# Second channel layer by seven block products also beside attention, with its sums in the mixing's two rooms

## The chip, the cores and the metric

The kernel runs on one core of one Trainium2 chip. The metric is the device time of one execution in microseconds, and the median of three runs stands for the kernel. One more execution was taken by the hardware profiler; all views and durations come from that one. Engines are PE (TensorE, matmuls), DVE (VectorE), ACT (ScalarE), POOL (GpSimd) and SP (the queue that issues DMAs). All data is fp32.

## What is computed

A masked attention over 4 batches, 8 heads, 768 positions and 64 features per head, then per batch a Fourier mixing and a two-layer network on the 768 x 512 result:

```python
scores = scale * np.matmul(q, k.transpose(0, 1, 3, 2))
scores = np.where(mask, scores, -1000000000.0)      # near blocks, edge blocks, sampled blocks
attn = np.exp(scores - np.max(scores, axis=-1, keepdims=True))
attn = attn / (np.sum(attn, axis=-1, keepdims=True) + 1e-09)
x = np.matmul(attn, v)                               # heads side by side: (4, 768, 512)

X = np.fft.fft(np.fft.fft(x, axis=1), axis=2)
u = x + np.real(X)
un = (u - mu) / np.sqrt(var + 1e-06)
out = u + np.maximum(un @ w_ch1, 0.0) @ w_ch2        # 512 -> 2048 -> 512
```

## The kernel before

**Attention** runs in 96 slots (`slot`), 24 for each batch: 4 pairs of heads, two halves of the 768 queries (384 each), and 6 key blocks of 128 in three slots of two units. For a unit PE makes scores (L578), ACT takes the exponential (L606), DVE multiplies by the mask into a tile `e` (L608), POOL adds `e` into `acc` for the row sums (L638), and PE multiplies `e` by the values two slots later (L652, `sum_up`). There are four `e` tiles and two PSUM banks for scores (pool `ps_s`). In the first batches' slots the mask is added on PE and there is no L608.

**The network of a batch runs while the next batch's attention does.** `begin(b)` makes the steps of batch b by `mixer`: a queue `apart` with the normalization (L761), the folds of the Fourier mixing, its products on PE (`zp`, `pq`), the arrivals in x (L926), the whitening `un` (L951), the transposes `utp` (L992) and the subtractions `right` (L1029); then a queue `late` with the two layers. The layers come in four rounds r. Each is two `quad`s (first layer: 512 of 2048 channels for all 768 tokens, by seven block products, L1075) and six `channels` steps (second layer: one of six blocks of 128 tokens, 4 matmuls of 128x512 at L1240, then one DVE add into x at L1243). For the last batch the second layer has a form of its own (`outputs`).

**A round of seven** replaces the six `channels` steps of a round. Its three token rounds (`round_of`, one for 128 tokens of both halves) each make seven products of 128x256 (L1183) in place of eight such blocks. Before these, `sums_room` takes its tiles and `round_right` makes four differences of weight blocks (128x512, POOL, L1152); for each token round `round_left` makes four sums of hidden blocks (two on DVE at L1168, two on POOL at L1165), ACT copies three partial products out of PSUM (`keep`, L1188), and three of the adds into x run on POOL (`later`, L1196), the rest on DVE (`plus` L1192, the double add L1222). The two open products of a token round, `yz` and `yw`, lie in the banks of the scores (`ps_s`). The sums and differences lie in the four `e` tiles, which attention must have left: `sums_room` calls `drain()`, which does the outstanding value products first.

So a round of seven is chosen only with `state["alone"]`. That is set by `until`, which runs all of `late` to its end when a place needs a batch's x finished (in the slots that follow the first ones of batches 2 and 3, and after the last slot): attention stands still there, and the mixing of the next batch runs in the gaps. Round 3 of a batch is always plain. Of the nine rounds 0 to 2 of batches 0 to 2, five go by seven: all three of batch 0, the third of batch 1, the third of batch 2.

**The order of the work** is made while the program is written out, by a model of each engine's time (`when`, `busy`): a wrong estimate moves an instruction in the order, and nothing at run time. After each step of `late`, `gap` takes steps of `apart` that fit by the model; for a DVE step that is `AHEAD` or `start` (from `state["soon"]`) of lead over PE. Beside attention `slot` takes steps of `late` at a pace `(us - COVER) / left`: `us` is the PE time of what lies in `late`, `left` the slots until attention must stand still, and `COVER` = 100 us is what is kept for that stretch. The mixing's rooms `big0` and `big1` (128 x 1536 fp32 each) hold its folds and, later, parts of its products; they lie unused while a batch's layers run and the next mixing has not begun.

Of the kernel before, what the change touches and what calls it, by code (L numbers as in the profile page):

```python
# [11 lines left out]
FP32 = mybir.dt.float32  # L12
# [5 lines left out]
ALU = mybir.AluOpType  # L18
# [81 lines left out]
def kernel(  # L100
# [14 lines left out]
    nc = tc.nc  # L115
# [862 lines left out]
    def mixer(b, xA, xB):  # L978
# [75 lines left out]
        def quad(p):  # L1054
# [5 lines left out]
            if not last:  # L1060
                if p % 2 == 0:
                    seven[p // 2] = state["alone"] and p // 2 < NF // 4 - 1
                elif seven[p // 2]:
                    state["drain"]()
                    sums_room()
                    for j in (1, 2, 4, 3):
                        round_right(p // 2, j)
# [55 lines left out]
            if last:  # L1123
                for j in ((1, 2), (3, 4))[p % 2]:
                    output_right(p // 4, j, p // 2 % 2)
            elif p % 2 == 1 and seven[p // 2]:
                state["soon"] = 0.4

        seven = {}
        w_t, h_s, kept = {}, {}, {}  # L1130

        def sums_room():

            def cut(t, at, k):
                return t[:, at:at + 2 * HS // 3 * k].rearrange("p (k n) -> p k n", k=k)

            rooms = [ep.tile([P, 2 * HS], FP32, tag="e", name="of") for _ in range(4)]
            w_t[1] = wt_p.tile([P, 2, DH], FP32, tag="wt", name="wt")
            for t, j in zip(rooms, (2, 3, 4)):
                w_t[j] = t[:, 0:2 * DH].rearrange("p (k n) -> p k n", n=DH)  # L1140
            for t, j in zip(rooms, (1, 3, 4)):
                h_s[j] = t[:, 2 * DH:2 * HS].rearrange("p (k n) -> p k n", n=P)
            for i in range(3):
                kept[i] = rooms[3][:, i * DH:(i + 1) * DH]

        def part(r, k, n):
            return w2_sb[:, 4 * r + 2 * k:4 * r + 2 * k + 2, n * DH:n * DH + DH]

        def round_right(r, j):
            a, c = {1: (part(r, 0, 1), part(r, 0, 0)), 2: (part(r, 1, 1), w_t[1]),  # L1150
                    3: (part(r, 1, 1), part(r, 0, 1)), 4: (part(r, 1, 0), w_t[2])}[j]
            nc.gpsimd.tensor_tensor(out=w_t[j], in0=a, in1=c, op=ALU.subtract)  # L1152
            busy("POOL", 1.35)

# [3 lines left out]

        def round_left(m, j):
            a11, a12, a21, a22 = tokens(m)  # L1160
            to, a, c, op = {1: (h_s[1], a21, a22, ALU.add), 2: (a21, h_s[1], a11, ALU.subtract),
                            3: (h_s[3], a22, a21, ALU.subtract),
                            4: (h_s[4], a12, a21, ALU.subtract)}[j]
            if j > 2:
                nc.gpsimd.tensor_tensor(out=to, in0=a, in1=c, op=op)  # L1165
                busy("POOL", 0.75, when["DVE"])
            else:
                tt(out=to, in0=a, in1=c, op=op)  # L1168
                busy("DVE", 0.43)

        def round_of(r, m):

            after = dict(zip(OUT, OUT[1:])).get(m)
            a11, a12, a21, a22 = tokens(m)
# [20 lines left out]
            def later(to, i, at):  # L1195
                nc.gpsimd.tensor_add(out=to, in0=kept[i], in1=to)  # L1196
                busy("POOL", 0.75, at)

            def ahead(*js):
                if after is not None:  # L1200
                    for j in js:
                        round_left(after, j)

            if m == OUT[0]:
                round_left(m, 1)
                round_left(m, 2)
            c_at, at = ps_m.tile([P, 512], FP32, tag="m", name="yc")[:, 0:DH], bank("m")
# [6 lines left out]
            if m == OUT[0]:  # L1214
                round_left(m, 3)
                round_left(m, 4)
            gap(start=0.9)
            k1 = keep(1, u_at, product(u_at, a21, w_t[2], False, k0))
            later(a1, 1, k1)
# [7 lines left out]
            ahead(1, 2, 3, 4)  # L1227
            state["soon"] = 1.6

        def channels(r, half, m):  # L1230

            if seven.get(r):
                round_of(r, m)
                if m == OUT[-1]:
                    for _ in range(T):
                        late.popleft()
                return
            y, at = ps_m.tile([P, DM], FP32, tag="m", name="y"), bank("m")
# [138 lines left out]
        for r in range(0 if last else NF // 4):  # L1377
# [9 lines left out]
    MOST, LEAST = 9.6, 2.5  # L1387
    COVER = 100.0
    AHEAD = 2.2
# [8 lines left out]
    state = {"paired": False, "total": None, "w": 0, "got": 0, "owed": 0.0, "ready": 0.0,  # L1398
             "alone": False, "drain": lambda: None}

    def channel_step():
        late.popleft()[0]()

# [58 lines left out]
    def until(met, alone=False):  # L1462

        state["alone"] = alone
        while not met():
            if late:
                channel_step()
                soon = state.pop("soon", None)
                gap(2.0, start=soon)
            else:  # L1470
                do_apart()
        state["alone"] = False

    def begin(b):


        before, after, rest = mixer(b, x_of[b, 0], x_of[b, 1])
# [303 lines left out]
```

## Time and profile before

| | |
|---|---|
| median of three runs | 1064.9 us (1064.24 to 1064.95) |
| profiled execution: its time, its span | 1066.03 us, 1064.3 us |
| mean granted PE clock | 0.987 |
| scores, L578 and values, L652, PE busy | 155.3 and 146.1 us |
| plain channel steps, L1240, matmuls x336, PE busy | 74.8 + 74.5 us |
| token rounds, L1183, matmuls x420 (15 token rounds) | 15.4 to 15.7 us for each of seven products |
| POOL adds of the row sums, L638, x204 | 211.6 us, some 1.06 us each |
| DVE mask multiply, L608, x88 | 79.9 us, 0.948 us each |

A matmul of the program is two instructions on PE in the trace. The span is from the first to the last instruction; the time of an execution also holds what lies around it. Busy times of matmuls overlap by a few tenths at their ends, so the price of a step is taken from one start to the next. The granted clock says which share of the full rate PE was given; it is 1.00 nearly throughout, and half of that in a few stretches of 3.4 or 6.8 us.

The stretches of the run, from the PE timeline: attention of batches 0 and 1 to some 246 us, the first standstill with all of batch 0's layers to 398, attention beside batch 1's layers to 554, the second standstill to 652, attention beside batch 2's layers to some 800, the third standstill with the last mixing to 908, then the last batch's layers alone.

### The profile page before, as it was taken

How to read it: one execution, taken by the hardware profiler on the slowest of the kernel's cores; microseconds unless marked ns; L12 is line 12 of the kernel's file. 1: busy time of each engine (PE TensorE's matmuls, PEld its weight loads, DVE VectorE, ACT ScalarE, POOL GpSimd, SP SyncE). 2: the span in 40 equal slices, each digit the busy share in tenths (PEclk: the TensorE clock that was granted, in tenths of full speed). 3: DMA queues.
4: the chain of work that ended last, by engine and by line, in shares of the span. 5: the costliest groups of instructions: out<-in, count | busy, mean ns of one | idle time of the engine just before them, and what ended most of it. 6: DMA issues, size and time to landing. Idle time of an engine off the chain costs nothing.

```text
span 1064.3 us, 13217 instructions
## 1 busy us (share of the span) xinstructions
PE 1026.7 (96%) x4594; PEld 572.3 (54%) x4594; DVE 708.7 (67%) x1287; ACT 382.5 (36%) x781; POOL 328.3 (31%) x365
## 2 busy tenths in 40 slices
PE   8999999999999998899999999799999999999996
PEld 4333345445766853444444764353445764578575
DVE  6898795877776566754668476765447736675663
ACT  6978765563222214342430223333221221210210
POOL 1000183556733404545561222645440401000000
PEclk9999999999999999999999999999999999899998
DMA  7857422220000002212120001311000002000001
GB/s 211 229 170 225 107 46 45 45 46 15 1 1 1 1 20 69 38 38 32 35 54 0 1 1 39 67 28 24 8 15 1 1 1 57 3 1 1 1 17 47
DMA packets 120549, 46.32 MB, mean 44 GB/s; under 512 B 108172, under 2 KB 113562, under 8 KB 120474
## 3 DMA queue, kind: packets, MB, share of 16 engines
q1 hardware_dynamic: 119222, 44.66, 17.6%
q10 hardware_dynamic: 1220, 0.72, 0.3%
q8 instruction: 38, 0.62, 0.2%
q14 instruction: 37, 0.30, 0.1%
q0 software_dynamic: 32, 0.01, 0.0%
HBM read 36.72 MB, written 6.29 MB: 40 GB/s over the span
## 4 chain that ended last, share of the span: by engine, by line
PE 84%; DVE 5%; ACT 4%; POOL 2%; issue 2%; DMA 1%; SPq 1%; ACTq 0%; DVEq 0%; POOLq 0%
PE z L1075 15%; PE y L1240 13%; PE s L578 12%; PE o L652 10%; PE yp L1075 7%; PE yy L1308 7%; PE xp L1075 4%; PE yz L1183 3%; PE yw L1183 2%; PE yc L1183 2%; PE zp L856 2%; PE s L588 1%; POOL acc L638 1%; ACT e L598 1%; PE sp L719 1%
## 5 line engine op out<-in xcount | busy, mean ns | idle before, releaser
L638 POOL TENSOR_TENSOR acc<-acc,e 128x384 f32<-128x384 f32 x158 | 162.6, 1062 | 97.0 <-DVE e L608 77.9
L578 PE MATMUL s<-qT,kT 64*128 64x384 f32 x768 | 155.3, 519 | 7.6 <-ACT e L598 5.2
L652 PE MATMUL o<-e,vr 128*64 128x384 f32 x768 | 146.1, 508 | 5.0 <-DVE oT L660 5.0
L638 POOL TENSOR_TENSOR acc<-e 128x384 f32<-128x384 f32 x46 | 49.0, 1084 | 202.4 <-ACT e L598 126.0
L578 PEld LDWEIGHTS s<-qT,kT 64*128 64x128 f32 x768 | 64.7, 188 | 86.5 <-ACT e L598 23.1
L608 DVE TENSOR_TENSOR e<-s,mask 128x768 f32<-128x768 f32 x88 | 79.9, 948 | 46.2 <-ACT s L606 35.6
L606 ACT ACTIVATE s<-s 128x768 f32<-128x768 f32 x88 | 66.8, 791 | 106.1 <-PE s L578 105.7
L598 ACT ACTIVATE e<-s 128x768 f32<-128x768 f32 x104 | 79.0, 809 | 49.0 <-PE s L588 36.5
L1075 PE MATMUL z<-unT,t 128*128 128x384 f32 x256 | 93.4, 488 | 1.6 <-DVE hA L1080 1.6
L652 PEld LDWEIGHTS o<-e,vr 128*64 128x64 f32 x768 | 48.5, 139 | 77.0 <-issue 67.5
L1080 DVE TENSOR_TENSOR hA<-z,hA 128x384 f32<-128x384 f32 x64 | 35.6, 557 | 70.0 <-PE z L1075 70.0
L1084 ACT ACTIVATE hA<-hA 128x384 f32<-128x384 f32 x64 | 33.5, 523 | 123.7 <-DVE hA L1080 123.7
L1240 PE MATMUL y<-w_sb,hA 128*128 128x512 f32 x168 | 74.8, 595 | 0.0
L1240 PE MATMUL y<-w_sb,hB 128*128 128x512 f32 x168 | 74.5, 595 | 0.0
L1196 POOL TENSOR_TENSOR x<-of,x 128x256 f32<-128x256 f32 x45 | 34.9, 783 | 123.2 <-ACT of L1188 83.4
L1075 PEld LDWEIGHTS z<-unT,t 128*128 128x128 f32 x256 | 48.3, 190 | 36.9 <-DVE hA L1080 4.0
L1243 DVE TENSOR_TENSOR x<-y,x 128x512 f32<-128x512 f32 x42 | 29.0, 691 | 57.3 <-PE y L1240 57.3
L1084 ACT ACTIVATE hB<-hB 128x384 f32<-128x384 f32 x64 | 33.5, 523 | 87.2 <-DVE hB L1080 87.2
L1240 PEld LDWEIGHTS y<-w_sb,hB 128*128 128x128 f32 x168 | 31.2, 190 | 38.2 <-issue 38.2
L1240 PEld LDWEIGHTS y<-w_sb,hA 128*128 128x128 f32 x168 | 31.1, 190 | 37.5 <-issue 36.7
L1075 PE MATMUL xp<-unT,w_sb 128*128 128x384 f32 x128 | 49.0, 506 | 0.0
L1075 PE MATMUL z<-t,w_sb 128*128 128x384 f32 x128 | 46.6, 487 | 0.2 <-DVE e L608 0.2
(235 smaller groups left out, 1728.5 us busy)
## 6 DMA issues: line engine op xcount, KB each, us to landing
wraw<-in_moe_w_ch_dram SPq DMA_DIRECT2D x32, 512.0 KB
vr<-in_v_dram SPq DMA_DIRECT2D x30, 192.0 KB
qb<-in_q_dram SPq DMA_DIRECT2D x44, 96.0 KB
kb<-in_k_dram SPq DMA_DIRECT2D x44, 96.0 KB
x<-oT SPq DMA_DIRECT2D x192, 12.0 KB
out_dram<-x SPq DMA_DIRECT2D x11, 252.0 KB
out_dram<-x SPq DMA_DIRECT2D x18, 128.0 KB
qr<-in_q_dram SPq DMA_DIRECT2D x24, 64.0 KB
```

The costliest lines, as they stand in the source:

```text
L578: nc.tensor.matmul(s[:, i, 0:HS], kT[rows, c * P:(c + 1) * P], qT[rows, queries], start=True, stop=u not in by_pe)
L598: nc.scalar.activation(out=e, in_=s[:, :, 0:HS], func=ACT.Exp, scale=scale)
L606: nc.scalar.activation(out=s[:, :, 0:HS], in_=s[:, :, 0:HS], func=ACT.Exp, scale=scale)
L608: nc.vector.tensor_tensor(out=e, in0=s[:, :, 0:HS], in1=m.broadcast_to([P, 2, HS]), op=ALU.mult)
L638: nc.gpsimd.tensor_add(out=acc[:, i, :], in0=start[:, i, :], in1=e[:, i, :])
L652: nc.tensor.matmul(o[D * i:D * i + D, :], vt[:, i, c, :], e[:, i, :], start=(c == 0), stop=(c == C - 1))
L1075: nc.tensor.matmul(to, a[:, k, :], c[:, k, :], start=(k == 0), stop=(k == ND // 2 - 1))
L1080: tt(out=to, in0=ps, in1=a, op=ALU.add)
L1084: nc.scalar.activation(out=h, in_=h, func=ACT.Relu)
L1183: nc.tensor.matmul(to, a[:, k, :], c[:, k, :], start=start and k == 0, stop=k == 1, skip_group_check=True)
L1240: nc.tensor.matmul(y, hs[0, half][:, l, m * P:(m + 1) * P], w2_sb[:, 4 * r + l, :], start=(l == 0), stop=(l == 3))
L1308: nc.tensor.matmul(ps, a[:, k, :], c[k // 2][:, k % 2, :] if isinstance(c, list) else c[:, k, :], start=(k == 0), stop=(k == 3))
```

## The change

The choice of a round moves into `choose`. A round 0 to 2 goes by seven with the `e` tiles when attention stands still, as before. Beside attention it now goes by seven too, with `"big"`: its sums then lie in the mixing's two rooms, cut into halves, and `drain` is not called; only when the next mixing's queue `apart` is empty, since the mixing needs these rooms. `choose` also replaces the six channel steps of such a round in `late` by three of 6.1 us, so that the pace counts them rightly. `state["open"]` counts the four steps from the second quad on, and `begin` runs them to their end before a new mixing starts.

In a round with `"big"` all subtractions, lefts and late adds run on DVE (`aside`). In the other rounds of seven the lefts 1 and 2 of the first token round move from DVE to POOL (`sooner` False); in the later token rounds they stay on DVE. The model's estimates for these steps are new ones by size. `state["soon"]`, which limits what `gap` puts in, is now reset before each step and is not set behind a round's last token round nor behind a quad. `COVER` goes from 100 to 117.

Counted in the built program: 72 fewer PE matmuls of 128x512 and 126 more of 128x256; DVE has 18 plain adds fewer and 80 other instructions more; ACT 27 copies more; POOL 31 instructions more; DMAs as before. Rounds of seven: batch 0 all three (attention still), batch 1 the first (beside attention) and the third (still), batch 2 the first (beside) and the second and third (still).

```diff
@@ -1059,10 +1059,9 @@
                     hs[g, i] = room((2, 0)[g] + i, [P, 4, HS], "h" + "AB"[i])
             if not last:
                 if p % 2 == 0:
-                    seven[p // 2] = state["alone"] and p // 2 < NF // 4 - 1
+                    choose(p // 2)
                 elif seven[p // 2]:
-                    state["drain"]()
-                    sums_room()
+                    sums_room(seven[p // 2])
                     for j in (1, 2, 4, 3):
                         round_right(p // 2, j)
             l1, l2 = 2 * (p % 2), 2 * (p % 2) + 1
@@ -1123,18 +1122,32 @@
             if last:
                 for j in ((1, 2), (3, 4))[p % 2]:
                     output_right(p // 4, j, p // 2 % 2)
-            elif p % 2 == 1 and seven[p // 2]:
-                state["soon"] = 0.4
 
         seven = {}
         w_t, h_s, kept = {}, {}, {}
 
-        def sums_room():
-
-            def cut(t, at, k):
-                return t[:, at:at + 2 * HS // 3 * k].rearrange("p (k n) -> p k n", k=k)
-
-            rooms = [ep.tile([P, 2 * HS], FP32, tag="e", name="of") for _ in range(4)]
+        def choose(r):
+
+            seven[r] = None
+            if r < NF // 4 - 1 and late:
+                seven[r] = "e" if state["alone"] else None if apart else "big"
+            if seven[r]:
+                quad_next = late.popleft()
+                for _ in range(2 * T):
+                    late.popleft()
+                late.extendleft((lambda m=m: round_of(r, m), 6.1) for m in OUT[::-1])
+                late.appendleft(quad_next)
+                state["open"] = T + 1 if seven[r] == "big" else 0
+
+        def sums_room(where):
+
+            if where == "e":
+                state["drain"]()
+                rooms = [ep.tile([P, 2 * HS], FP32, tag="e", name="of") for _ in range(4)]
+            else:
+                state["open"] -= 1
+                both = [room(i, [P, T, DM], "of").rearrange("p t d -> p (t d)") for i in range(2)]
+                rooms = [b[:, i * 2 * HS:(i + 1) * 2 * HS] for b in both for i in range(2)]
             w_t[1] = wt_p.tile([P, 2, DH], FP32, tag="wt", name="wt")
             for t, j in zip(rooms, (2, 3, 4)):
                 w_t[j] = t[:, 0:2 * DH].rearrange("p (k n) -> p k n", n=DH)
@@ -1143,33 +1156,40 @@
             for i in range(3):
                 kept[i] = rooms[3][:, i * DH:(i + 1) * DH]
 
+        def aside(r, out, a, c, op, n, at=0.0, sooner=False):
+
+            if seven[r] == "big" or sooner:
+                tt(out=out, in0=a, in1=c, op=op)
+                return busy("DVE", n * 0.0011 + 0.15, at) + HOP
+            nc.gpsimd.tensor_tensor(out=out, in0=a, in1=c, op=op)
+            return busy("POOL", n * 0.0026 + 0.07, at) + HOP
+
         def part(r, k, n):
             return w2_sb[:, 4 * r + 2 * k:4 * r + 2 * k + 2, n * DH:n * DH + DH]
 
         def round_right(r, j):
             a, c = {1: (part(r, 0, 1), part(r, 0, 0)), 2: (part(r, 1, 1), w_t[1]),
                     3: (part(r, 1, 1), part(r, 0, 1)), 4: (part(r, 1, 0), w_t[2])}[j]
-            nc.gpsimd.tensor_tensor(out=w_t[j], in0=a, in1=c, op=ALU.subtract)
-            busy("POOL", 1.35)
+            aside(r, w_t[j], a, c, ALU.subtract, 2 * DH)
 
         def tokens(m):
             return [hs[0, i][:, 2 * k:2 * k + 2, m * P:(m + 1) * P]
                     for i in range(2) for k in range(2)]
 
-        def round_left(m, j):
+        def round_left(r, m, j, sooner=True):
             a11, a12, a21, a22 = tokens(m)
             to, a, c, op = {1: (h_s[1], a21, a22, ALU.add), 2: (a21, h_s[1], a11, ALU.subtract),
                             3: (h_s[3], a22, a21, ALU.subtract),
                             4: (h_s[4], a12, a21, ALU.subtract)}[j]
-            if j > 2:
-                nc.gpsimd.tensor_tensor(out=to, in0=a, in1=c, op=op)
-                busy("POOL", 0.75, when["DVE"])
-            else:
-                tt(out=to, in0=a, in1=c, op=op)
-                busy("DVE", 0.43)
+            left_at[j] = aside(r, to, a, c, op, DH, left_at.get(2 if j > 2 else 1, 0.0) if j > 1
+                               else when["PE"], sooner and j < 3)
+
+        left_at = {}
 
         def round_of(r, m):
 
+            if state["open"]:
+                state["open"] -= 1
             after = dict(zip(OUT, OUT[1:])).get(m)
             a11, a12, a21, a22 = tokens(m)
             a0, a1 = xA[:, m, 0:DH], xA[:, m, DH:DM]
@@ -1193,17 +1213,16 @@
                 return busy("DVE", 0.43, done) + HOP
 
             def later(to, i, at):
-                nc.gpsimd.tensor_add(out=to, in0=kept[i], in1=to)
-                busy("POOL", 0.75, at)
+                aside(r, to, kept[i], to, ALU.add, DH, at)
 
             def ahead(*js):
                 if after is not None:
                     for j in js:
-                        round_left(after, j)
+                        round_left(r, after, j)
 
             if m == OUT[0]:
-                round_left(m, 1)
-                round_left(m, 2)
+                for j in (1, 2):
+                    round_left(r, m, j, False)
             c_at, at = ps_m.tile([P, 512], FP32, tag="m", name="yc")[:, 0:DH], bank("m")
             a_at = plus(a0, c_at, product(c_at, a12, part(r, 1, 0), True))
             give(at, a_at - HOP)
@@ -1212,10 +1231,10 @@
             o_at, at = ps_m.tile([P, 512], FP32, tag="m", name="yc")[:, 0:DH], bank("m")
             give(at, plus(b0, o_at, product(o_at, a22, w_t[4], True)) - HOP)
             if m == OUT[0]:
-                round_left(m, 3)
-                round_left(m, 4)
+                for j in (3, 4):
+                    round_left(r, m, j, False)
             gap(start=0.9)
-            k1 = keep(1, u_at, product(u_at, a21, w_t[2], False, k0))
+            k1 = keep(1, u_at, product(u_at, a21, w_t[2], False, max(k0, left_at[2])))
             later(a1, 1, k1)
             k2 = keep(2, d_at, product(d_at, h_s[1], w_t[1], True, z_at[1]))
             done = product(u_at, h_s[3], w_t[3], False, k1)
@@ -1225,16 +1244,11 @@
             later(b1, 2, max(z_at[0], k2))
             z_at[1] = plus(a1, d_at, product(d_at, h_s[4], part(r, 1, 1), False, k2))
             ahead(1, 2, 3, 4)
-            state["soon"] = 1.6
+            if after is not None:
+                state["soon"] = 1.6
 
         def channels(r, half, m):
 
-            if seven.get(r):
-                round_of(r, m)
-                if m == OUT[-1]:
-                    for _ in range(T):
-                        late.popleft()
-                return
             y, at = ps_m.tile([P, DM], FP32, tag="m", name="y"), bank("m")
             for l in range(4):
                 nc.tensor.matmul(y, hs[0, half][:, l, m * P:(m + 1) * P], w2_sb[:, 4 * r + l, :],
@@ -1385,7 +1399,7 @@
 
 
     MOST, LEAST = 9.6, 2.5
-    COVER = 100.0
+    COVER = 117.0
     AHEAD = 2.2
     ALONE = 3.0
     LEAVES = 9.0
@@ -1396,9 +1410,10 @@
     asked = set()
     needed = set()
     state = {"paired": False, "total": None, "w": 0, "got": 0, "owed": 0.0, "ready": 0.0,
-             "alone": False, "drain": lambda: None}
+             "alone": False, "drain": lambda: None, "open": 0, "soon": None}
 
     def channel_step():
+        state["soon"] = None
         late.popleft()[0]()
 
     def behind(kind):
@@ -1465,14 +1480,16 @@
         while not met():
             if late:
                 channel_step()
-                soon = state.pop("soon", None)
-                gap(2.0, start=soon)
+                gap(2.0, start=state["soon"])
             else:
                 do_apart()
         state["alone"] = False
 
     def begin(b):
 
+        while state["open"]:
+            channel_step()
+            gap()
 
         before, after, rest = mixer(b, x_of[b, 0], x_of[b, 1])
         any_of = len(late) + len(apart) + 4 * len(rest)
```

## The prediction

> **What bounds it now.** First the page, its busy times and the chain of waits: is one engine full, or do several take turns?
>
> ```profile
> span 1064.3 us, 13217 instructions
> PE 1026.7 (96%) x4594; PEld 572.3 (54%) x4594; DVE 708.7 (67%) x1287; ACT 382.5 (36%) x781; POOL 328.3 (31%) x365
> PE 84%; DVE 5%; ACT 4%; POOL 2%; issue 2%; DMA 1%; SPq 1%; ACTq 0%; DVEq 0%; POOLq 0%
> ```
>
> PE (TensorE) is busy for 1026.7 of 1064.3 us, so only two things can move the end: PE work, and the 37.6 us in which PE stands. Then PE's timeline: what does each kind of step cost when nothing holds it?
>
> ```profile
> 554.86 10.57 PE L1240 MATMUL y<-w_sb,hA 128*128 128x512 f32 x24
> 565.26 10.46 PE L1240 MATMUL y<-w_sb,hB 128*128 128x512 f32 x24
> 575.57 1.45 PE L1075 MATMUL xp<-unT,w_sb 128*128 128x384 f32 x4
> ...
> 838.65 1.03 PE L1183 MATMUL yc<-w_sb,hA 128*128 128x256 f32 x4
> 844.69 1.03 PE L1183 MATMUL yc<-w_sb,hA 128*128 128x256 f32 x4
> ```
>
> A start to the next start is the price. Six plain channel steps take 20.71 us (554.86 to 575.57); one token round of seven products takes 6.04 (838.65 to 844.69), three 18.12, and 18.62 with their waits (832.12 to 850.74, where the next step begins). Last the stretches by window, for the places where PE stands:
>
> ```profile
> 441.00:554.00 113.00, 111.47 (x463) 50.48 (x464) 65.61 (x95) 45.56 (x89) 54.22 (x57) 1.00 0.23 42
> 695.00:800.00 105.00, 104.13 (x405) 47.34 (x404) 53.27 (x85) 31.25 (x56) 47.30 (x48) 1.00 0.11 19
> 436.00:440.00 4.00, 3.75 (x14) 1.47 (x16) 3.33 (x4) 0.00 (x0) 2.81 (x3) 0.57 0.08 12
> ```
>
> ```profile
> PE utp L992 <- DVE un L951: 5.5, 5, 1.9
> PE o L652 <- DVE oT L660: 5.0, 2, 2.5
> PE utp L992 <- DVE sums L701: 1.5, 2, 0.7
> ```
>
> (Columns of a window: its length, then busy us of PE, PEld, DVE, ACT, POOL, then the granted clock.) Beside attention with plain steps PE is full and DVE (VectorE) 51 to 58% busy. PE stands at three seams, where a mixing ends and attention resumes: 398 to 441 (5.5 us idle), 652 to 695 (5.7) and 800 to 912 (3.1). The seams cost more than that: the clock is 0.57 from 436 to 440, right behind the 2.51 us wait for oT, 0.57 from 422 to 426 behind the waits of 0.73 and 1.94, 0.50 from 689 to 692 and 0.50 from 904 to 910.
>
> **What the change does.** The instruction order of both built programs shows that it takes effect: PE loses 72 of the 128x512 matmuls (18 channel steps) and gains 126 of 128x256 (9 token rounds). Rounds of seven products go from 5 to 8: the first round of batches 1 and 2 now goes that way beside attention, and batch 2's second one while attention stands still. Batch 1's second stays plain, since the next mixing is queued by then. No DMA is added or removed, and SP's count is unchanged.
>
> 1. **PE work removed.** Per round 20.71 less 18.12 to 18.62, so 2.1 to 2.6; I take 2.4. Three rounds: **-7.2 us** (-6.3 to -7.8), all on the path, as PE sets the end.
>
> 2. **Two rounds beside attention.** There DVE takes over what POOL does in the others. DVE has nearest rows: 0.685 for 128x512 (L1276), 0.42 for 128x256 (L1192), 0.686 for the double add (L1222). A round is 4x0.685 + 3x(4x0.42 lefts, 3x0.42 laters, 3x0.42 sums, 0.69) = 17.4, less six plain adds of 0.69: +13.3 us. In the 441-554 stretch that makes 79 of some 110 us: it fits, so the price is in the order, not in the load. In the quad at 510.97 the score multiplies end at 513.15; four subtractions then end at 515.9, the first sum at 516.5, and the product that reuses its PSUM tile wanted 516.23: 0.4 us. In a token round PE's second product takes over the score bank: 0.87 after the scores end by PE, 1.3 by the first multiply: 0.45 each, six times. In batch 1's first one a 0.97 transpose and two lefts stand behind the multiplies, so the fourth product, ready at 3.05, waits until 4.0: 0.95. Sum 2x0.4 + 6x0.45 + 0.95 = **+4.5**. Bounds: 0, if it goes like the quads beside attention today (waits of 0.24 and 0.57 in all), and 26.6, if none of the added DVE time is hidden.
>
> 3. **Rounds with attention still, now six.** The first token's first two lefts move from DVE (0.51 and 0.43) to POOL (0.89 by L1165, 0.83). They start when the quad's last sum and relu are done (0.1+0.56+0.1+0.52, about 1.3 us after PE leaves the quad), end at 3.2, and the fourth product is ready at 2.6: 0.6 each. 6x0.6, less the 0.6 that today's five lose to POOL: **+3.0** (0 to 6). POOL's four subtractions of 1.50 stay under the 9.05 us quad.
>
> 4. **The seams.** The order moves mixing forward against attention. After batch 0 all whitening but the last is ahead of the first scores, and half of the eight subtractions of L1029 (7.2 us per batch, four of them directly ahead of the oT transpose today) are issued earlier: I take out 1.94 and 2.51, and one half-clock stretch of 3.4 us, worth 1.7. After batch 1 the last whitening stays late, so I count half of 1.93 and 2.51: 2.2. Before the final stage one more plain step (3.45) stands between the last mixing product and the first transpose; of 1.7 us of waits for un there I take 1.5. Together -9.9. Against it: in the second standstill the folds (3.7+2.1+1.4+2.8+2.6 = 12.6 us by their rows, and some 3 of adds) have about 13 us of plain steps to hide in where they had 25: +2.5. And two slots in a row without channel work leave POOL 8x2.1 = 17 us of sums in 12.6 us of PE (four times 1.49 and 1.44, and 0.85); four tiles of e absorb most: +1. Net **-6.4** (-14 to +6: all three seams empty with their half-clock stretches, or none better and both new waits twice as long).
>
> The Trainium skill ("TensorE: Matmul & The Clock Gate", Part 1) lets the clock fall after an idle window of about 3.4 us, and its closing table allows pauses up to about 3 us; no pause at these seams is that long, the longest 2.51, yet the clock halved there, so the trace speaks against reading it as one single pause. By that reading the 1.7 would drop out of the sum and give 1060.5, inside the forecast's own range and with no chance of its own.
>
> **Sum:** -7.2 + 4.5 + 3.0 - 6.4 = -6.1. The profiled execution took 1066.0 (span 1064.3 and 1.7 around it), the median is 1064.9; the difference applies to either, so **1058.8**.
>
> **Rivals.**
> - *The seams stay as they are* (part 4 is 0): the waits for un and oT hang on DVE's queue, which is no shorter. For it: the wait after the sums (0.73, twice) is in the new order as before. Against it: the oT transpose has fewer subtractions directly ahead. -7.2+4.5+3.0 = +0.3: 1065.2, no change. Chance 0.15.
> - *DVE's order sets the pace beside attention* (slower): behind each token round DVE still holds four lefts and late sums, 2.6 us by my walk, so the next score multiplies come late, the score banks with them, and PE pauses twice, around 2.7 us per round, enough for a half-clock stretch as at 436. For it: DVE goes from 58 to 71%, and everything there passes one queue; against it: values lag two slots and need no fresh e. Six rounds of 2.7 plus 1.7 of clock are 26 in place of 4.5, half the seams kept: -7.2+26.4+3.0-3.2 = +19, 1084; it decides the sign from some 11 us of such waits on. Chance 0.18 for any of it that ends slower.
> - *All goes well*: no waits beside attention and the seams empty with their clock: -7.2+1-12 = -18, 1047. Everything must fit at once. Chance 0.07.
>
> **How the numbers follow.** My forecast, 1052.7 to 1062.7, has 0.60; its edges are part 2 at 2 with part 4 at -10 (-12.2), and part 2 at 5 with part 4 at -3 (-2.2). A measurement of this kernel can tell some 0.2% (2.1 us) from no change. Faster: 0.60, 0.07 and 0.03 of the first rival: 0.70; same 0.12; slower 0.18. The range for 8 in 10 is 1052 to 1068: below it most of the last rival, above it most of the slower one.
>
> **What would show it.** Right: PE busy some 7 us lower; the waits of L652 on oT and of the transposes on un smaller; waits under 1 us on PE's second and fourth product in the token rounds beside attention, and on POOL's lefts in the others; no new half-clock stretch. Wrong: score matmuls that wait for DVE's multiply behind each such round, a clock under 1 in these windows, or the seams' waits unchanged.

## The result, and the profile after

The changed kernel takes 1080.05 us (median of six runs, 1075.43 to 1082.27) against 1064.44 us for the kernel before in the same session (six runs, 1063.6 to 1064.95). The ratio is 1.014 with a 95% interval of 1.0117 to 1.0163: slower by 15.6 us. The profiled execution took 1080.02 us with a span of 1078.2, so it stands for the median.

The page of the changed kernel, its span and busy times:

```profile
span 1078.2 us, 13625 instructions
PE 1022.8 (95%) x4702; PEld 592.1 (55%) x4702; DVE 736.8 (68%) x1349; ACT 393.7 (37%) x808; POOL 357.4 (33%) x396
```

PE does less than before (1022.8 us busy against 1026.7) and stands longer: 55.4 us of the span against 37.6. Its busy time fell by 3.9 us, where the prediction looked for some 7, and far more than that came back as waits. The table of PE's waits says for whom (total us, times, longest):

```profile
PE z L1074 <- DVE hA L1079: 11.8, 6, 3.0
PE s L578 <- DVE e L608: 7.3, 8, 1.3
...
PE yz L1203 <- POOL of L1164: 4.0, 5, 1.2
PE yz L1203 <- POOL hB L1164: 2.9, 5, 0.7
...
PE utp L992 <- DVE un L951: 2.5, 4, 0.8
PE yz L1203 <- DVE e L608: 2.0, 3, 0.9
PE peak_row L1663 <- DVE peak L1661: 1.9, 1, 1.9
```

The two waits for `oT` (5.0 us before) are gone and the transposes' waits for `un` fell from 5.5 to 2.5: the seams emptied. Grown are the waits of quads for their first sum (11.8, where 1.6 stood before), of token rounds for lefts on POOL (6.9 in all, before 0.6), and of the scores for DVE's multiply (7.3, before 2.1). All rows of the table sum to 45.6 us, those of the kernel before to 27.7. The windows that the prediction showed, and two of 3.4 us:

```profile
441.00:554.00 113.00, 104.24 (x481) 52.76 (x480) 82.74 (x122) 46.49 (x93) 60.85 (x60) 1.00 0.24 42
695.00:800.00 105.00, 98.17 (x430) 52.96 (x431) 72.68 (x119) 35.44 (x65) 51.62 (x51) 0.98 0.11 19
756.90:760.30 3.40, 3.40 (x13) 1.99 (x12) 2.07 (x4) 1.59 (x2) 3.40 (x4) 0.64 0.00 0
828.60:832.00 3.40, 3.20 (x6) 1.83 (x7) 2.39 (x6) 0.52 (x1) 0.00 (x0) 0.64 0.00 0
```

Beside attention PE stood 1.5 and 0.9 us before; now 8.8 and 6.8: 13.2 us more in the windows where the rounds with `"big"` run. Two stretches of half clock are new, behind a wait of 1.91 us (`peak_row`) and one of 3.00 (a quad's `z`); those at the first two seams are gone (the granted clock is 1.00 from 398 to 441 and from 652 to 700). A token round with attention still costs what it did when nothing holds it (6.05, from 808.39 to 814.44).

Why DVE is late beside attention is seen in its timeline at the head of a second quad (start, duration, engine, line, operation, and in brackets a wait):

```profile
459.34 6.23 POOL L638 TENSOR_TENSOR acc<-acc,e 128x384 f32<-128x384 f32 x6
463.98 0.74 DVE L1162 TENSOR_TENSOR wt<-w_sb 128x512 f32<-128x512 f32 x1
464.75 1.37 DVE L1162 TENSOR_TENSOR of<-w_sb,wt 128x512 f32<-128x512 f32 x1
465.54 2.84 POOL L638 TENSOR_TENSOR acc<-e 128x384 f32<-128x384 f32 x2
466.16 1.37 DVE L1162 TENSOR_TENSOR of<-w_sb,of 128x512 f32<-128x512 f32 x1
467.45 1.48 DVE L1162 TENSOR_TENSOR of<-w_sb 128x512 f32<-128x512 f32 x1
469.45 1.56 PE L1074 MATMUL z<-unT,t 128*128 128x384 f32 x4 [2.15 <-DVE hA L1079]
```

The four subtractions take 4.96 us, not the 2.74 that four of 0.685 make, and PE waits 2.15 in place of 0.4. All four run while POOL adds up row sums (L638), one add right behind the other, yet the first takes 0.74 and the others twice that. What differs is how much of the running add is left when a subtraction starts. The add that began at 463.16 took 1.01, so the first subtraction started 0.19 us ahead of its end. The next add began at 464.12 and took 1.46. Its end, 465.58, is 0.83 us behind the start of the second subtraction, which takes 0.69 longer than the 0.68 of a subtraction with POOL idle. POOL pays too: this add meets the first subtraction and takes 1.46 in place of 1.00. Behind a token round the same is seen with the lefts:

```profile
495.81 0.41 DVE L1162 TENSOR_TENSOR of<-hB 128x256 f32<-128x256 f32 x1
496.06 2.15 POOL L638 TENSOR_TENSOR acc<-e 128x384 f32<-128x384 f32 x2 [10.44 <-PE sp L733]
496.26 1.10 DVE L1162 TENSOR_TENSOR hB<-of,hA 128x256 f32<-128x256 f32 x1
497.40 1.10 DVE L1162 TENSOR_TENSOR of<-hB 128x256 f32<-128x256 f32 x1
498.42 1.23 DVE L1162 TENSOR_TENSOR of<-hA,hB 128x256 f32<-128x256 f32 x1
501.03 1.46 PE L578 MATMUL s<-qT,kT 64*128 64x384 f32 x6 [0.86 <-DVE e L608]
```

The first left starts before POOL's adds do and takes 0.41; the next three start with 0.81 to 0.95 us of an add left and take 1.10 to 1.23; the mask multiply (L608) queues behind them and the scores wait for its bank. Not every DVE operation pays. Two of the same shape, both in the middle of POOL's adds, 0.8 us apart:

```profile
504.63 0.41 DVE L1212 TENSOR_TENSOR x<-yc,x 128x256 f32<-128x256 f32 x1
505.24 1.00 POOL L638 TENSOR_TENSOR acc<-acc,e 128x384 f32<-128x384 f32 x1
505.48 1.04 DVE L1162 TENSOR_TENSOR x<-of,x 128x256 f32<-128x256 f32 x1 [0.43 <-ACT of L1208]
```

The one that reads PSUM (`yc`) takes its usual 0.41; the one that reads two SBUF tensors takes 1.04, with 0.76 of the add left. The trace of the kernel before had the same pair of prices in one line of the code, in two places (its timeline, L1029 with POOL adding and, at the end, without):

```profile
426.69 5.21 POOL L638 TENSOR_TENSOR acc<-acc,e 128x384 f32<-128x384 f32 x4 [5.17 <-DVE e L608]
428.16 1.48 DVE L1029 TENSOR_TENSOR unT<-unT 128x512 f32<-128x512 f32 x1
...
908.77 0.68 DVE L1029 TENSOR_TENSOR unT<-unT 128x512 f32<-128x512 f32 x1
```

So 1.48 and 0.68 for the same subtraction were there to be read. The prediction read L1029 as a sum of 7.2 us for eight and took its price for the new operations from rows where POOL stood still or one operand was in PSUM.

The Trainium skill ("SBUF — State Buffer", section "Who interferes with whom") says that a VectorE instruction with two SBUF inputs contends with a GpSimd instruction that reads SBUF, that one with at most one SBUF input and outside the two-port modes does not, and that the one that comes second is blocked until the first is done. The trace agrees, and its rows give the size: a DVE operation with two SBUF operands that starts during an add of POOL takes its own time and what is left of the add, less 0.13 to 0.14 us (0.69 more with 0.83 left, 0.62 more with 0.76 left, 0.06 more with 0.19 left). In a row of such operations each one holds up POOL's next add (1.17 to 1.46 in place of 1.00) and the following one then waits for it: 0.41 becomes 1.10 and 0.68 becomes 1.37.

### The profile page after: what moved, and what is told of

Same layout as the page of the kernel before. It is cut to its first block, busy times and chain, and to the rows that moved or that the text cites. A ratio compares the mean times of both kernels' runs of the same rounds, so it can differ in the third digit from the quotient of the medians.

```text
span 1078.2 us, 13625 instructions
## 1 busy us (share of the span) xinstructions
PE 1022.8 (95%) x4702; PEld 592.1 (55%) x4702; DVE 736.8 (68%) x1349; ACT 393.7 (37%) x808; POOL 357.4 (33%) x396
## 5 line engine op out<-in xcount | busy, mean ns | idle before, releaser
L638 POOL TENSOR_TENSOR acc<-acc,e 128x384 f32<-128x384 f32 x158 | 163.2, 1067 | 74.7 <-DVE e L608 55.6
L652 PE MATMUL o<-e,vr 128*64 128x384 f32 x768 | 143.0, 499 | 0.0
L638 POOL TENSOR_TENSOR acc<-e 128x384 f32<-128x384 f32 x46 | 51.7, 1143 | 197.2 <-ACT e L598 126.2
L1074 PE MATMUL z<-unT,t 128*128 128x384 f32 x256 | 94.3, 491 | 11.8 <-DVE hA L1079 11.8
L608 DVE TENSOR_TENSOR e<-s,mask 128x768 f32<-128x768 f32 x88 | 79.9, 949 | 37.0 <-ACT s L606 33.9
L939 POOL TENSOR_SCALAR st<-st 128x1 f32<-128x1 f32 x24 | 8.4, 350 | 135.1 <-DVE st L938 134.8
L1164 POOL TENSOR_TENSOR x<-of,x 128x256 f32<-128x256 f32 x54 | 40.6, 760 | 28.2 <-DVE x L1241 11.4
L1208 ACT COPY of<-yz 128x256 f32<-128x256 f32 x48 | 17.9, 372 | 87.3 <-PE yz L1203 82.1
L1164 POOL TENSOR_TENSOR of<-hB 128x256 f32<-128x256 f32 x24 | 22.6, 943 | 80.5 <-ACT hB L1083 69.6
L1074 PE MATMUL yp<-unT,w_sb 128*128 128x384 f32 x128 | 47.5, 495 | 0.5 <-DVE un L912 0.5
L1074 PE MATMUL yp<-t,w_sb 128*128 128x384 f32 x128 | 47.6, 495 | 0.0
```

The lines of the kernel that those rows point to most:

```text
L608: nc.vector.tensor_tensor(out=e, in0=s[:, :, 0:HS], in1=m.broadcast_to([P, 2, HS]), op=ALU.mult)
L638: nc.gpsimd.tensor_add(out=acc[:, i, :], in0=start[:, i, :], in1=e[:, i, :])
L652: nc.tensor.matmul(o[D * i:D * i + D, :], vt[:, i, c, :], e[:, i, :], start=(c == 0), stop=(c == C - 1))
L1074: nc.tensor.matmul(to, a[:, k, :], c[:, k, :], start=(k == 0), stop=(k == ND // 2 - 1))
L1164: nc.gpsimd.tensor_tensor(out=out, in0=a, in1=c, op=op)
L1208: nc.scalar.copy(out=kept[i], in_=src)
```

## The experiments

All are edits of the changed kernel if nothing else is said; times are medians, ratios stand against the kernel before on the same chip. Three questions: is the loss in the rounds beside attention, in those with attention still, or in the order (the pace, the limits of `gap`)? What makes DVE late beside attention? And can the losses be mended so that the seams' gain is left?

**The lefts of a first token back on DVE.**

```diff
                 for j in (1, 2):
-                    round_left(r, m, j, False)
+                    round_left(r, m, j)
```

> The changed kernel with one thing undone: the first token's lefts 1 and 2 in the rounds with attention still are on DVE again. Theory A (the loss has three parts of like size: POOL's lefts, the folds in the quads, the rounds beside attention): the waits of yz on POOL, some 8.5 us in six such rounds, fall to 1 to 2, so about 1074. Rival B (the rounds beside attention are the whole loss): 1079 to 1081.

1083.61 us, ratio 1.0165 (1.014 to 1.019): no better. The waits for POOL went and came back under DVE's name:

```profile
PE yz L1203 <- DVE hB L1162: 7.4, 6, 1.7
```

There the lefts stand behind the quad's sums and the mixing's operations. Neither forecast held (1074, or 1079 to 1081). Moving the lefts to POOL was not what made these rounds slow.

**Both limits of `gap` as before.**

```diff
+            elif p % 2 == 1 and seven[p // 2]:
+                state["soon"] = 0.4
...
-            if after is not None:
-                state["soon"] = 1.6
+            state["soon"] = 1.6
```

> The changed kernel with the limits of gap as before: 1.6 behind every token round, 0.4 behind a second quad of seven. Theory A: both waits of 3.0 us in a quad of the first and third standstill go (6 to 8 us with the clock), but the order at the seam behind batch 0 is again that of the kernel before (7 us lost there) and no plain step is left between the last mixing product and its transposes (3 to 5 lost): 1080 to 1085. Rival (these limits matter nowhere): 1080, with the 3.0 us waits still there. Rival C (the folds are the main loss and the seams gained nothing): 1072.

1080.71, ratio 1.0153 (1.0131 to 1.0175): no change in sum, but the waits trade places. The waits of 3.00 in a quad are gone, and PE's waits for lefts on POOL fall from 6.9 to 0.9. The seams' waits are back:

```profile
PE utp L992 <- DVE un L951: 8.1, 5, 3.8
...
PE o L652 <- DVE oT L660: 4.7, 2, 2.5
```

Of the 8.1 us, 6.1 lie ahead of the last stage, where the kernel before waited 1.7. What a looser limit takes out of a seam it puts into a quad and into the lefts: the same operations of the mixing, at an earlier place in DVE's queue. In the changed kernel three of DVE's adds (L761, from 268.05) run beside the first two lefts on POOL, which take 0.88 and 1.05 us; with the limits back DVE starts them behind the lefts, and these take 0.73 each.

**No rounds of seven beside attention**, the rest of the change kept.

```diff
-                seven[r] = "e" if state["alone"] else None if apart else "big"
+                seven[r] = "e" if state["alone"] else None
```

> The changed kernel without the two rounds beside attention, their steps plain again; six rounds of seven. Theory A: PE has 4.8 us more work, and the waits in these two stretches go (two quads 2.1 each, token rounds 5.8, scores behind them 4 to 5, the flag 1.9): about 1070. Rival B (they are the whole loss): 1062 or less. Rival D (they are a gain and the standstills lose): 1083.

1068.13, ratio 1.0032 (1.0021 to 1.0043). The two rounds beside attention cost 11.9 us net (1080.05 less 1068.13). The rows of this kernel's table of PE's waits sum to 33.3 us, so 12.3 of the changed kernel's 45.6 go with these rounds: 4.3 in the quads, 3.5 of scores behind the multiply, 2.0 of second products, 1.6 for `peak_row`, the rest small. Two rows and the windows of this kernel:

```profile
PE z L1074 <- DVE hA L1079: 7.5, 4, 3.0
...
PE s L578 <- DVE e L608: 3.8, 5, 1.2
```

```profile
441.00:554.00 113.00, 110.35 (x462) 49.77 (x461) 69.63 (x99) 43.75 (x86) 59.55 (x62) 1.00 0.24 42
695.00:800.00 105.00, 103.03 (x422) 50.40 (x421) 60.20 (x96) 32.50 (x58) 50.58 (x53) 1.00 0.10 18
```

PE idles 4.6 us in both together, where the changed kernel idles 15.6. What the rounds save is small beside that: their six token rounds take 40.5 us of PE from start to start, waits taken out, and the twelve plain steps in their place 42.8. So 2.2 us are saved, not the 4.8 of the prediction's price.

**The pace alone**: the kernel before with its `COVER` at 117.

```diff
-    COVER = 100.0
+    COVER = 117.0
```

> The kernel before with COVER 117 in place of 100 and nothing else; one more round of seven with attention still, six in all. Its PE order has the seam behind batch 0 as before and the later ones as in the changed kernel. If the seam behind batch 1 gains by the pace: 1064.4 less 2.4 for the round, less 2 to 4 for the seam, plus 3 to 5 at the end where no plain step is left ahead of the transposes: 1062 to 1066. If the pace alone cost what the change lost: 1075 or more.

1067.43, ratio 1.0029 (1.0018 to 1.004), though it gains a round of seven; neither range held. The transposes ahead of the last stage wait 6.1 us for `un`, where the kernel before waited 1.7. The changed kernel, with 1.7 there, doesn't have this loss.

**Without POOL's row sums** in batches 2 and 3, with and without rounds beside attention. This part of the computation is left out: `acc` is only started, not added to.

```diff
-            for i in range(2):
+            for i in range(2 if c == 1 or n < 2 * NP else 0):
                 nc.gpsimd.tensor_add(out=acc[:, i, :], in0=start[:, i, :], in1=e[:, i, :])
```

> The changed kernel, with POOL's adds of the row sums left out beyond the first of each half for the attention of batches 2 and 3 (so that the output isn't the reference's); all other instructions and PE's order stay. Theory F (a DVE operation with two SBUF operands takes twice as long while POOL adds): the subtractions beside attention fall from 1.4 to 0.7 us, the lefts behind a token round from 1.1 to 0.42, the two waits of 2.15 in the quads to some 0.4, and the excess over the same cut without rounds beside attention falls from 12 to 0 to 4 us. Rival G (the order of DVE's queue alone): durations as they are, excess 9 to 12.

> The kernel without rounds beside attention, with the same adds of the row sums left out. It is the base for the run before: by theory F it gains little, 1 to 4 us against 1068, since plain steps hold no DVE operation of two SBUF operands; by rival G the same.

1072.99 (ratio 1.0076, 1.0057 to 1.0096) and 1065.57 (1.0005, 0.9994 to 1.0017). The rounds beside attention now cost 7.4 us instead of 11.9, between the two forecasts (0 to 4, and 9 to 12). So some 4.5 us are owed to the adds that were left out; by the four intervals this difference is good to 3 or 4 us. In the timeline of the first, the two subtractions that start during POOL's one remaining pair of adds are slow; the one that starts ahead of the pair and the one behind it are not:

```profile
463.20 0.68 DVE L1162 TENSOR_TENSOR wt<-w_sb 128x512 f32<-128x512 f32 x1
463.36 2.77 POOL L638 TENSOR_TENSOR acc<-e 128x384 f32<-128x384 f32 x2 [6.53 <-DVE e L608]
463.92 1.37 DVE L1162 TENSOR_TENSOR of<-w_sb,wt 128x512 f32<-128x512 f32 x1
465.32 1.37 DVE L1162 TENSOR_TENSOR of<-w_sb,of 128x512 f32<-128x512 f32 x1
466.61 0.68 DVE L1162 TENSOR_TENSOR of<-w_sb 128x512 f32<-128x512 f32 x1
467.81 1.56 PE L1074 MATMUL z<-unT,t 128*128 128x384 f32 x4 [1.22 <-DVE hA L1079]
```

This shows the slowing and what makes it. It doesn't split the loss cleanly: two of the four subtractions are still slow, and the quad waits 1.22, where the prediction's walk with four fast ones had 0.4.

**The subtractions spread** over both quads, two at each one's end, still on DVE.

```diff
...
+            elif seven[p // 2] == "big":
+                if p % 2 == 0:
+                    sums_room("big")
+                for j in ((1, 2), (4, 3))[p % 2]:
+                    round_right(p // 2, j)
...
```

> The changed kernel with the four weight subtractions of a round beside attention moved from the head of its second quad to the ends of both quads, two each. PE's order stays. If their place ahead of the quad's first sum is what costs: the waits of 2.15 and 2.14 go, 1075 to 1076. If the load on DVE decides, they come back as waits of the scores or the token rounds: 1079 to 1081.

1076.02, ratio 1.0098 (1.0067 to 1.013). The two quad waits of 2.15 and 2.14 are gone (that row falls from 11.8 to 7.5), and the median falls by 4.0. The intervals of the two ratios overlap, so the size rests on the trace.

**The late adds of these rounds on POOL**, to take load off DVE.

```diff
             def later(to, i, at):
-                aside(r, to, kept[i], to, ALU.add, DH, at)
+                nc.gpsimd.tensor_add(out=to, in0=kept[i], in1=to)
```

> The changed kernel with the three late adds of each token round beside attention on POOL, as in the other rounds; lefts and subtractions stay on DVE. DVE has 18 adds of 0.42 to 1.1 us less: if its load behind the token rounds is what costs, the waits there (0.9 and 0.25 on the score bank, 0.86 and 1.9 behind them) halve: 1077. If POOL's adds then make row sums late, or slow DVE as much: 1080 or more.

1096.66, ratio 1.0301 (1.0279 to 1.0323). The adds stand behind row sums on POOL; DVE's next add into the same x waits for them, and the score matmuls behind that:

```profile
505.03 0.42 DVE L1212 TENSOR_TENSOR x<-yw,x 128x256 f32<-128x256 f32 x1 [8.16 <-POOL x L1216]
505.51 1.65 PE L578 MATMUL s<-qT,kT 64*128 64x384 f32 x4 [6.88 <-DVE x L1212]
```

So the change's choice of DVE for these adds was the better of the two.

**Mending the rounds with attention still.** First, without rounds beside attention, the first token's lefts 3 and 4 right behind 1 and 2 on POOL, ahead of the late adds.

```diff
-                for j in (1, 2):
+                for j in (1, 2, 3, 4):
                     round_left(r, m, j, False)
...
-            if m == OUT[0]:
-                for j in (3, 4):
-                    round_left(r, m, j, False)
```

> The version without rounds of seven beside attention (1068.1), and for a round's first token the lefts 3 and 4 stand on POOL right behind the lefts 1 and 2, ahead of the late adds. Nothing of the computation is left out. Theory: in the rounds with attention still, PE's waits for POOL (0.4 to 1.2 us each, 6.9 us in all) come from the order on POOL's queue; the five waits on `of` (4.0 us) go, the five on hB stay at about 0.5 each: 1063 to 1065. Rival: POOL is simply too slow there for four lefts, wherever they stand, or the earlier lefts hold up DVE's adds: the waits move by name and the time stays at 1067 to 1069.

1062.1 (1058.93 to 1066.47), ratio 0.9976 (0.9961 to 0.9992): 6.0 us less than the version without it (1068.13). The five waits on `of` (4.0) are gone, and those on hB stay at 2.8. The two profiled executions differ by only 3.1 us (1066.71 and 1063.65), so the gain is clear and its size isn't.

**Then the limit of 1.6 behind the last token round too**, with and without the rounds beside attention (the second with the subtractions spread).

```diff
-            if after is not None:
-                state["soon"] = 1.6
+            state["soon"] = 1.6 if after is not None else 1.6
```

> As the run before, and the limit of 1.6 for what is put in behind a round is set behind the last token round too (not behind the quads, where none is set, as in the change). Nothing of the computation is left out. Theory: the two waits of 3.00 us in a quad came because five fold operations stand together on DVE ahead of the quad's first sum; spread over two steps they cost under 1 us each, and the seams' gain, which rests on the order behind the quads, stays: 1057 to 1061, faster than the kernel before. Rival: the seams' waits for oT and un (2 to 2.5 us each) come back as they did when both limits were put back: 1064 to 1068.

> The change with all its eight rounds of seven, the subtractions beside attention spread over both quads, the lefts 3 and 4 ahead of the late adds on POOL, and the limit of 1.6 behind the last token round. Nothing of the computation is left out. Theory (the rounds beside attention cost more than they save, by DVE's slowed operations on two SBUF tensors and the score multiplies behind them, about 8 us also with the subtractions spread): 7 to 9 us above the run before, 1064 to 1070. Rival (with the order mended the saved PE work of 4.8 us shows): at or below the run before, 1053 to 1060.

1065.36 (ratio 1.0004, 0.9995 to 1.0013): the rival held, as the waits for `oT` (4.7) and `un` (7.5) came back. With the rounds beside attention 1074.41 (1.0092, 1.0076 to 1.0107): 9.05 us more, where the theory had 7 to 9. With the order mended these rounds still lose. How these 9 us divide between slowed operations and DVE's queue behind the token rounds, no run shows.

**Last, one fold fewer in the quad**: the limit behind the last token round at 2.6, without rounds beside attention.

```diff
-            if after is not None:
-                state["soon"] = 1.6
+            state["soon"] = 1.6 if after is not None else 2.6
```

> The version of 1062.1 (no rounds beside attention, all four lefts ahead of the late adds on POOL) with the limit behind the last token round set so that one fold operation fewer (the second of L788, 0.95 us alone and 2.0 beside POOL) stands on DVE ahead of the quad's first sum; the order behind the quads, and with it the seams, stays nearly as it is. Nothing of the computation is left out. Theory: a quad's wait is the folds ahead of its first sum, so the two waits of 3.00 us fall by 1.0 to 2.0 each, and the waits for oT stay away: 1057 to 1061. Rival: the wait or the seams' waits turn up elsewhere in the same size, since DVE's work is only shifted: 1062 to 1066.

1059.37 (1058.1 to 1060.85), ratio 0.9954 (0.994 to 0.9968): faster than the kernel before. Its interval overlaps that of the version of 1062.1 (0.9961 to 0.9992), and one wait for `oT` (2.2 us) came back, so the step between the two is less sure than the gain on the kernel before. The timeline of the version of 1062.1, where the quad waits 3.00:

```profile
287.54 1.98 POOL L1164 TENSOR_TENSOR wt<-w_sb 128x512 f32<-128x512 f32 x1
...
289.73 1.23 DVE L796 COPY e<-x 128x2 f32<-128x2 f32 x1
...
292.48 2.01 DVE L788 TENSOR_TENSOR sd<-sd 128x765 f32<-128x765 f32 x1
...
295.01 1.56 PE L1074 MATMUL z<-unT,t 128*128 128x384 f32 x4 [3.00 <-DVE hA L1079]
```

and the same quad in the version of 1059.37:

```profile
291.37 1.56 PE L1074 MATMUL z<-unT,t 128*128 128x384 f32 x4 [1.06 <-DVE hA L1079]
...
296.35 0.95 DVE L788 TENSOR_TENSOR sd<-sd 128x765 f32<-128x765 f32 x1
```

One operation of 2.01 us left the head of the quad, and the wait fell by 1.94. Some us later, with POOL's subtractions done, it takes 0.95. The collision with POOL is the one from beside attention: in the version of 1062.1 the five operations ahead of the first sum take 7.1 us beside POOL's four subtractions (287.30 to 294.41); by their rows with POOL idle they take 3.0. An estimate from this: without the collision DVE would be through by 290.3, before the product that the first sum needs is done (at some 290.7), and the wait of 3.00 wouldn't be there. No run tests that.

## Why the prediction was wrong

The forecast was 1058.8 us and faster; it came out at 1080.05. By its own steps:

1. **PE work removed, -7.2: right in sign, less than half the size.** Between 240 us and the last stage the plain steps of the second layer fell from 146.1 to 83.0 us and the token rounds rose from 91.9 to 152.0 (from each matmul's start to the next one's, waits over 0.15 us taken out): 3.0 less. A still token round does cost the 6.05 foreseen. Beside attention one costs 6.5 to 6.8, and 7.6 in the stretch of half clock. The prediction took its price where attention stands still and used it for all three rounds; the two beside attention save 2.2, not 4.8.

2. **Two rounds beside attention, +4.5: the step that failed.** The mechanism was named rightly (a quad's product behind the subtractions, the second product behind the multiply) but mis-sized: the waits that go with these rounds are 12.3 us by the two tables, and 11.0 by the idle time of the two windows. DVE's durations, priced at 0.685 and 0.42, became 1.37 and 1.10 beside POOL's row sums, so "the price is in the order, not in the load" left out a third thing, what POOL does meanwhile; by the runs without row sums that is some 4.5 us. The walk through the quad then gives 2.15 instead of 0.4; the place of the subtractions costs 4.0, and the two figures overlap. The waits in token rounds on the second product came at 0.92, 0.25 and 0.85 and on the fourth at 0.61, near the 0.45 and 0.95 foreseen. What the sum did not hold is the scores behind the lefts (their waits for the multiply are 7.3 us in all, and 3.8 in the run without these rounds), and a wait of 1.91 for `peak`, with a stretch of half clock behind it. That was the slower rival's place, priced there at 26.4.

3. **Lefts on POOL, +3.0: right in kind, half the size.** The trace has 6.9 us of such waits against the 0.6 of today, and undoing the order of the lefts 3 and 4 gained 3 to 6. The prediction walked the lefts 1 and 2 (0.71, 0.44, 0.55 on hB, near its 0.6) and left out that 3 and 4 queue behind late adds (up to 1.22 on `of`). The move to POOL alone is cheap: with the limits of `gap` put back these waits are 0.9.

4. **The seams, -6.4: the gain larger, and its price larger and elsewhere.** Behind batch 0 the lost time (waits, and half of each half-clock stretch) fell from 8.9 to 1.7 us, behind batch 1 from 7.4 to 2.7: 11.9 gained, where 8.4 of the 9.9 were laid on these two. The 1.5 at the end did not come (6.4 before and after). Against it stood +2.5 for folds in the second standstill; they cost nothing there, but 3.00 in a quad of the first and of the third, and half a clock once: some 7. The +1 for POOL's sums is not in the table of waits. Net some -5.

With about -3, +12, +6 and -5 this makes +10 of the profiled execution's +14.0 (1080.02 less 1066.03); the rest is spread over small waits and not assigned.

Of the rivals, the slower one (DVE's order sets the pace beside attention, 1084) is what happened in sign. That its time came so near is luck: its term beside attention was 26.4 where some 12 came, and the rest of the loss lies in the standstills, of which it had 3.0. Its argument against itself, that values need no fresh `e`, did not help: the scores need the bank that the multiply frees.

## What to carry to other kernels

Price a DVE operation by the company it will keep: read the minimum and the maximum of its row, and what POOL does in each, before taking a duration from an idle place. For one that reads two SBUF tensors beside a busy POOL, add what is left of POOL's running instruction; in a row of them that is most of one instruction each. When work moves to an engine that has spare time on average, list what stands behind each moved operation in its queue; here a left of 0.42 us was harmless by load and cost a score matmul its bank. And look for the place to which a removed wait's work went: the limit that emptied the seams filled a quad, and the best version (1059.37) came without the rounds beside attention, from the places of a few operations.

## What the hardware showed unexpectedly

- What a DVE operation loses beside POOL doesn't depend on its own size. Beside POOL's 128x512 subtractions, in the version of 1062.1, a copy of 128x2 (L796) went from 0.16 to 1.23 us and a 128x765 operation (L788) from 0.95 to 2.01: 1.07 and 1.06 more, each with 1.2 us of a subtraction left when it started. The copy has one SBUF operand, so one operand is not always safe.
- One pause of PE doesn't decide the clock. In the changed kernel two equal waits of 3.00 us stand ahead of the same quad product; behind the one at 828.80 the clock is 0.64 on the mean of 3.4 us, behind the one at 295.18 it is 1.00. A wait of 1.91 (756.47) was enough for 0.64 as well. By this trace's clock records the half-clock stretches of 71.77, 757.85 and 829.53 begin whole multiples of 3.413 us apart (201 and 222 times). Laid on that grid, the stretches ahead of these two points and the two that share the pause ahead of 295.18 look so:

```profile
290.23:293.64 3.41, 1.95 (x7) 0.80 (x5) 3.38 (x3) 0.00 (x0) 3.33 (x3) 1.00 0.00 0
293.64:297.05 3.41, 1.87 (x6) 1.21 (x7) 3.34 (x7) 0.52 (x1) 0.20 (x1) 1.00 0.00 0
754.44:757.85 3.41, 1.50 (x11) 0.77 (x9) 2.31 (x6) 0.21 (x1) 3.41 (x5) 1.00 0.02 4
826.12:829.53 3.41, 0.73 (x2) 0.49 (x3) 3.38 (x5) 0.16 (x1) 1.34 (x1) 1.00 0.00 0
```

PE is busy for 1.50 and 0.73 us ahead of the two falls, and for 1.95 and 1.87 where the grid divides the pause and the clock stays. That fits a clock that goes by PE's work in fixed stretches and not by a pause; no run tests it, and the limit isn't sharp (914.86 to 918.28, with 1.77 busy, is followed by half clock).
